# An attention and Fourier kernel: the planner's allowance for late transfers goes by engine instead of by operation

## The chip, the cores and the metric

The kernel runs on one core of a Trainium2 chip. The metric is the device time in microseconds (us), from three runs. A core has TensorE (PE in the profile, its weight loads PEld), VectorE (DVE), ScalarE (ACT), GpSimd (POOL) and SyncE (SP), which here issues every transfer. Each engine works through its own queue in the order in which the program was written for it; engines wait for one another by semaphores.

## The reference

Two independent branches read their own input and their outputs are put side by side: full attention with 32 heads of width 32, and a Fourier mixing layer written as four products with cosine and sine matrices.

```python
# A_x (1, 2048, 1024), wqkv (1024, 3072), wo (1024, 1024)
qkv = (x @ wqkv).reshape(B, S, 3, 32, 32).transpose(2, 0, 3, 1, 4)
scores = einsum("bhqd,bhkd->bhqk", q, k) * 32 ** -0.5
o = einsum("bhqk,bhkd->bhqd", softmax(scores), v)
a = o.transpose(0, 2, 1, 3).reshape(B, S, D) @ wo
# B_x (1, 2048, 1024), dft_seq_* (2048, 2048), dft_hid_* (1024, 1024)
y = einsum("ts,bse->bte", seq_re, x @ hid_re.T) - einsum("ts,bse->bte", seq_im, x @ hid_im.T)
return concatenate([a, y], axis=-1)
```

All is float32.

## The kernel before

**The dense products** (the projections of x to q, k and v, the two Fourier products, the projection with wo) are computed by seven block products where eight would be usual, so many operands are sums or differences of blocks. Each operand goes through the same steps:

- SyncE loads a block of 128x512 numbers, 256 KB (`raw` or `er`; lines 486 and 854), and where a second or third block belongs to it, that one too (`g` or `raw`; line 495).
- An add or subtraction joins them (line 502). GpSimd or VectorE takes it.
- A rounding makes the high part (lines 522 and 523: ScalarE or VectorE); a subtraction of that from the whole makes the low part (line 526: GpSimd or VectorE). They are called `h`, `l` or, together, a `slot`.
- TensorE multiplies high with high, low with high and high with low (lines 416 and 438), 12 or 24 matmuls of 128x512 into one bank of PSUM (`pd` or `psT`). VectorE, in the first steps ScalarE too, evacuates the bank into sums (lines 676 to 792, 979 to 1019; ScalarE's are lines 775 and 790). These matmuls are called fills.

**Attention** runs head by head (heads are counted from 0), three streams at once. S: 32 pairs of score matmuls per head (line 1317), each 128x1024; VectorE takes the negated maximum of each row (`negm`, line 1323) and ScalarE the exponential with its sum (line 1326). Then the maxima of a head are split, transposed on VectorE (lines 1350 to 1360, `lt`), written to HBM (`m_d`) and read back as two more rows of `qs` (`qs<-m_d`, line 1365). T: 64 transposed score matmuls (line 1442), which need those rows, and their exponentials on ScalarE (line 1451). V: runs of matmuls of these with the values (line 1474), 20 to 32 in a row, whose result VectorE evacuates (lines 1494 and 1496).

**The order** is made while the program is built. `Plan` keeps a clock of its own and a time at which each engine is free. An operation (`Op`) names an engine, a cost in us and the operations it follows, and some name a second engine (`other`) that may take it instead. When all that it follows has been started, it is put into the pending list of each engine that may take it, with the time from which it may start; an engine that is free takes the one of the lowest rank among those whose time has come. The order in which the plan starts them is the order of the queues on the chip. An operation that has been put into a queue holds everything behind it there until what it needs is there.

The time from which an operation may start is the end of what it follows, plus 0.1 or 0.2 us, plus an allowance, `SLACK`, that goes by the engine it follows and the engine named first in the operation: 2.0 us after a transfer for GpSimd, VectorE and TensorE, and none for ScalarE. A rounding is named as VectorE's, with ScalarE as the other; ScalarE may take it only while `spare` is set, in the first steps (the first five of the projections' twelve) and in the projection with wo. An add is named as GpSimd's, with VectorE as the other.

TensorE's stream is chosen by the loop at the end. It starts a fill, a pair of S, a T or a run of V. A run of V is held back for up to `PATIENCE` us while work for ScalarE of less than `STOCK` us is waiting; S goes ahead of T while that work is more than `SFIRST`. Fills are handed out in proportion to what attention has done.

Of the kernel before, what the change touches and what calls it, by code (L numbers as in the profile page):

```python
# [38 lines left out]
class Op:  # L39


    __slots__ = ("engine", "cost", "emit", "rank", "kb", "other", "left", "ready", "end", "begun", "then", "soon", "lanes", "two")

    def __init__(self, engine, cost, emit, rank=0.0, kb=0, other=None, two=False):
        self.engine, self.cost, self.emit, self.rank, self.kb, self.other = engine, cost, emit, rank, kb, other
        self.left, self.ready, self.end, self.begun, self.lanes = 0, -1e3, None, False, 1
        self.then, self.soon = [], []
        self.two = two


class Ring:
# [14 lines left out]
class Plan:  # L66
# [5 lines left out]
    LAT_PE = 0.2  # L72
    OVERLAP = {"ACT": 0.15, "DVE": 0.08, "POOL": 0.08}

    SLACK = {("SP", "POOL"): 2.0, ("SP", "DVE"): 2.0, ("SP", "PE"): 2.0, ("POOL", "DVE"): 0.7}
    KB_US = 360.0
    LANDING = 1.6
    QUEUE = 1.0
# [35 lines left out]
    def _wait(self, o, d):  # L114
        if d.end is None:
            d.then.append(o)
            o.left += 1
        else:
            o.ready = max(o.ready, self.after(d, d.engine, o))

    def after(self, d, e, o):
        return d.end + (self.LAT_PE if e == "PE" else self.LAT) + self.SLACK.get((e, o.engine), 0.0)

    def _release(self, o):
        if o.engine != "PE":
            self.seq += 1
            heapq.heappush(self.pending[o.engine], (o.ready, self.seq, o.rank, o))
            if o.other:
                heapq.heappush(self.pending[o.other[0]], (o.ready, self.seq, o.other[2], o))

    def start(self, o, e=None):
        e = e or o.engine
        made = o.emit(e) if o.other else o.emit()
        o.begun = True
        self.free[e] = self.now + (o.cost if e == o.engine else o.other[1])
        if e == "POOL" or e == "DVE" and o.two:
            self.port = self.free[e]
        if e == "DVE" and o.two:
            self.held = made, self.free[e]
        elif e == "POOL" and self.held is not None and self.held[1] > self.now - self.NEAR:  # L140
            self.behind(made, self.held[0])
        if o.kb:
            for _ in range(o.lanes):
                t = max(self.free[e], self.lane[0])
                self.dma = max(self.dma, t) + o.kb / o.lanes / self.KB_US
                o.end = self.dma + self.LANDING
                self.lane = self.lane[1:] + [o.end]
                if o.lanes > 1:
                    self.free[e] = t + o.cost
        else:  # L150
            o.end = self.free[e]
            self.free[e] -= self.OVERLAP.get(e, 0.0)
        for t in o.then:
            t.ready = max(t.ready, self.after(o, e, t))
            t.left -= 1
            if t.left == 0:
                self._release(t)
        for t in o.soon:
            t.ready = max(t.ready, self.now)
            t.left -= 1  # L160
            if t.left == 0:
                self._release(t)
        o.then = o.soon = ()
        o.emit = None
# [56 lines left out]
def kernel(  # L221
# [150 lines left out]
    RES = 400  # L372
    SST = 12
    LEAD = 4
    PATIENCE = 0.5
    STOCK = 1.8
    NEAR = 0.2
    SFIRST = 1
    ADD = 0.68
    FILL = 3 * (7 * 24 * 4 + 7 * 16 * 4 + 7 * 8 * 16 + 2 * 8 * 4)  # L380
    ATT = H * (128 * MM + 16 * PV) + (3 * H2 + 2 * (H - H2)) * SWITCH
# [1 line left out]
    pl = Plan()  # L383
    pl.behind = lambda a, b: tc.add_manual_dep(a.ins, b.ins.name, mybir.DependencyInfo(mybir.DependencyClass.Sync, mybir.DependencyReason.DATA), reason="port")
    op = pl.op
    att_on, t_on = [True], [False]
# [1164 lines left out]
    while nf < len(fills) or any(place[n] < len(s) for n, s in streams.items()):  # L1551
        pl.others()
        if pl.free["PE"] > pl.now:
            pl.now = max(pl.now + 1e-3, min(pl.free["PE"], pl.next_time()))
            continue
        if visit:
            o = visit[0]
            if o.left == 0 and o.ready <= pl.now:
                pl.start(o)
                done += o.cost  # L1560
                visit.pop(0)
            else:
                t = min(pl.next_time(), o.ready if o.left == 0 else 1e18)
                assert t < 1e17, "the plan is stuck"
                pl.idle = getattr(pl, "idle", 0.0) + max(t - pl.now, 1e-3)
                pl.now = max(t, pl.now + 1e-3)
            continue
        heads = {n: s[place[n]] for n, s in streams.items() if place[n] < len(s)}
        if not heads:
            att_on[0] = False  # L1570
        banks = [e for e in banks if e.end is None or e.end + pl.LAT > pl.now]
        room = 0.0
        if len(banks) >= (2 if heads and t_on[0] else 4):
            room = max(pl.now + 1e-3, min([e.end + pl.LAT for e in banks if e.end is not None] or [1e18]))
        ok, times = [], [pl.next_time()]
        waiting = [e for e in waiting if not e.begun]
        stock = max(0.0, pl.free["ACT"] - pl.now) + sum(e.cost for e in waiting)
        held = False
        if "S" in heads and "T" in heads and heads["T"][0].left == 0:
            th, tk = heads["T"][1:3]  # L1580
            held = heads["S"][2] / 33.0 * SST + 16 * (heads["S"][1] - th - 1) - tk / 4 > LEAD
        for n, (o, h, k, *_) in heads.items():
            if o.left:
                continue
            ready = o.ready + LATE
            if n == "V":
                ready = max(ready, room)
            if ready > pl.now:
                times.append(ready)
                continue  # L1590
            if n == "V":

                near = any(m in heads and heads[m][0].left == 0 and heads[m][0].ready + LATE < pl.now + NEAR and not (m == "S" and held) for m in "ST")
                if (near or stock < STOCK) and pl.now < o.ready + PATIENCE:
                    times.append(o.ready + PATIENCE)
                    continue
            rank = {"V": 0, "T": 1, "S": 0.5 if stock > SFIRST else 1.5}[n]
            if n == "S" and "T" in heads and heads["T"][0].left == 0:
                th, tk = heads["T"][1:]
                lead = k / 33.0 * SST + 16 * (h - th - 1) - tk / 4  # L1600
                if lead > LEAD:
                    continue
                if lead > 0:
                    rank = 2
            ok.append((rank, n))
        fill = None
        if nf < len(fills):
            o, first, left = fills[nf]
            ready = o.ready if o.left == 0 else 1e18
            if first:  # L1610
                ready = max(ready, room)
            if ready + (LATE if first else 0.0) <= pl.now:
                fill = o
            elif ready < 1e17:
                times.append(ready + LATE)
        if fill is not None and (not ok or (not first and left <= HB) or nf / (FILL - RES) <= done / ATT):
            pl.start(fill)
            nf += 1
            if first:
                banks.append(frees[ng])  # L1620
                ng += 1
            continue
        if ok:
            n = min(ok)[1]
            o = heads[n][0]
            pl.start(o)
            place[n] += 1
            t_on[0] = t_on[0] or n == "T" or n == "S" and place["S"] > 31
            if n == "V":
                banks.append(heads[n][2])  # L1630
                visit = list(heads[n][3])
            elif o in exp_of:
                waiting.append(exp_of[o])
            done += o.cost
            continue
        t = min(times)
        assert t < 1e17, "the plan is stuck"
        pl.idle = getattr(pl, "idle", 0.0) + max(t - pl.now, 1e-3)
        pl.now = max(t, pl.now + 1e-3)
    while True:  # L1640
        pl.others()
        t = pl.next_time()
# [31 lines left out]
```

## Time and profile before

| | us |
| --- | --- |
| median of three runs | 2944.36 |
| lowest and highest | 2943.4 and 2950.26 |
| the profiled execution's own time | 2947.49 |
| its span, first to last instruction | 2945.7 |
| TensorE busy in the span | 2933.7 |
| VectorE, ScalarE, GpSimd busy | 2300.6, 2271.9, 907.5 |

The span is what the views of the profile cut into pieces; the 1.8 us between it and the execution's own time lie around it. A row of the timeline or of the chain of waits has its start and its length in us. In rows of groups the numbers behind the bar are the busy time, the mean of one in ns, and the idle time of the engine just before them with what ended it. A row "A <- B: x, n, y" of the waits says that A's engine was idle x us in total, n times, y at the longest, until B. Rows of the stages give the length of the stage, then the busy time of PE, PEld, DVE, ACT and POOL, the clock granted to TensorE, the share of the transfer engines and GB/s.

### The profile page before, as it was taken

To read this page: it belongs to the slowest core of one execution; us is meant where nothing else is said; L and a number is where in the kernel's file an instruction comes from. 1 tells how busy PE (TensorE), PEld (TensorE's weight loads), DVE (VectorE), ACT (ScalarE), POOL (GpSimd) and SP (SyncE) were. 2 spreads that over 40 slices of the span, in tenths; PEclk is the share of its full clock that TensorE was granted. 3 is DMA by queue.
4 is the path that set the end of the run, shared out by engine and by line. 5 is a ranking of instruction groups with operands and counts; after the bars stand their busy time and mean duration, and the time that the engine had idled before them with its cause. 6 is when DMAs were issued, how large, how long until landed. Compare 5 with 4: busy or idle time off the path is not lost.

```text
span 2945.7 us, 45665 instructions
## 1 busy us (share of the span) xinstructions
PE 2933.7 (100%) x14922; PEld 2149.6 (73%) x14922; DVE 2300.6 (78%) x3141; ACT 2271.9 (77%) x4321; POOL 907.5 (31%) x709
## 2 busy tenths in 40 slices
PE   9999999999999999999999999999999999999999
PEld 7887777677777777777777777776777766776787
DVE  6778888678877877777678888888777888887685
ACT  4348888888888888888888888888988888886331
POOL 2323336222213332232112543333122444342142
PEclk9999999999999999999999999999999999999999
DMA  9975658667636655665434776565434786655753
GB/s 349 365 237 182 193 184 286 208 214 236 219 109 225 215 177 166 206 231 166 140 111 154 244 230 199 184 195 153 135 112 133 220 264 215 198 179 181 241 201 127
DMA packets 393881, 587.97 MB, mean 200 GB/s; under 512 B 112782, under 2 KB 114574, under 8 KB 393518
## 3 DMA queue, kind: packets, MB, share of 16 engines
q1 hardware_dynamic: 393644, 585.05, 61.8%
q8 instruction: 120, 1.97, 0.3%
q14 instruction: 117, 0.96, 0.1%
HBM read 421.30 MB, written 163.59 MB: 199 GB/s over the span
## 4 chain that ended last, share of the span: by engine, by line
PE 96%; DMA 2%; DVE 1%; SPq 0%; issue 0%; ACT 0%; POOL 0%; DVEq 0%; ACTq 0%
PE pd L416 44%; PE psT L1442 16%; PE psS L1317 16%; PE pd L1474 15%; PE psT L416 6%; DMA qs<-m_d 0%; DVE negm L1323 0%; DMA er<-in_wqk 0%; PE psT L438 0%; DMA g<-in_wqk 0%; DMA raw<-in_wqk 0%; DMA er<-in_xa 0%; DMA g<-in_ct 0%; DMA ks<-qk_d 0%; DVE l L526 0%
## 5 line engine op out<-in xcount | busy, mean ns | idle before, releaser
L1323 DVE TENSOR_REDUCE negm<-psS 128x1 f32<-128x1024 f32 x1024 | 1242.1, 1220 | 239.6 <-PE psS L1317 234.1
L1326 ACT ACTIVATE psS<-psS,negm 128x1024 f32<-128x1024 f32 x1024 | 1219.1, 1190 | 134.3 <-DVE negm L1323 128.7
L416 PE MATMUL pd<-slot,h 128*128 128x512 f32 x3360 | 1147.2, 390 | 0.2 <-DVE ot L1496 0.2
L1451 ACT ACTIVATE pt<-psT 128x512 f32<-128x512 f32 x1296 | 775.0, 695 | 212.5 <-PE psT L1442 201.6
L1442 PE MATMUL psT<-qs,ks 128*128 128x512 f32 x2048 | 793.5, 393 | 1.2 <-DMA qs<-m_d 1.0
L416 PEld LDWEIGHTS pd<-slot,h 128*128 128x128 f32 x3360 | 630.8, 188 | 132.3 <-DVE ot L1496 0.6
L416 PE MATMUL pd<-slot,l 128*128 128x512 f32 x1680 | 654.6, 390 | 0.0
L1317 PE MATMUL psS<-ks,qs 128*128 128x512 f32 x1552 | 473.5, 390 | 1.9 <-ACT psS L1326 1.8
L1442 PEld LDWEIGHTS psT<-qs,ks 128*128 128x128 f32 x2048 | 379.8, 188 | 128.1 <-issue 41.8
L526 POOL TENSOR_TENSOR l<-raw,h 128x512 fp32r<-128x512 f32 x163 | 210.2, 1290 | 728.0 <-PE psT L1442 346.6
L502 POOL TENSOR_TENSOR raw<-raw,g 128x512 f32<-128x512 f32 x225 | 291.9, 1304 | 392.5 <-DVE raw L502 66.2
L416 PEld LDWEIGHTS pd<-slot,l 128*128 128x128 f32 x1680 | 315.4, 188 | 66.8 <-issue 0.8
L1474 PE MATMUL pd<-pt,vt 128*32 128x512 f32 x2592 | 345.8, 594 | 0.4 <-DVE slot L979 0.4
L1317 PEld LDWEIGHTS psS<-ks,qs 128*128 128x128 f32 x1552 | 290.5, 188 | 66.6 <-ACT psS L1326 4.7
L526 POOL TENSOR_TENSOR slot<-raw,slot 128x512 fp32r<-128x512 f32 x174 | 223.8, 1292 | 368.1 <-DVE slot L523 101.5
L1326 ACT ACTIVATION_READ_ACCUMULATOR psS<-psS,negm 128x1 f32 x1024 | 316.6, 309 | 0.0
L1451 ACT ACTIVATE ptm<-psT 128x512 f32<-128x512 f32 x392 | 237.5, 701 | 39.1 <-PE psT L1442 38.4
L1451 ACT ACTIVATE ptl<-psT 128x512 f32<-128x512 f32 x360 | 221.8, 705 | 35.2 <-PE psT L1442 33.2
L1474 PEld LDWEIGHTS pd<-pt,vt 128*32 128x32 f32 x2592 | 89.4, 110 | 180.9 <-issue 173.0
L416 PE MATMUL pd<-slot,slot 128*128 128x512 f32 x768 | 193.7, 390 | 0.0
L416 PEld LDWEIGHTS pd<-slot,slot 128*128 128x128 f32 x768 | 144.2, 188 | 31.0
L523 DVE CAST h<-raw 128x512 fp32r<-128x512 f32 x321 | 148.9, 465 | 16.8 <-PE pd L416 14.2
(138 smaller groups left out, 2362.5 us busy)
## 6 DMA issues: line engine op xcount, KB each, us to landing
raw<-in_ct SPq DMA_DIRECT2D x224, 256.0 KB
g<-in_ct SPq DMA_DIRECT2D x128, 256.0 KB
c<-u_d SPq DMA_DIRECT2D x120, 256.0 KB
qk_d<-e SPq DMA_DIRECT2D x52, 512.0 KB
qs<-qk_d SPq DMA_DIRECT2D x128, 192.0 KB
ks<-qk_d SPq DMA_DIRECT2D x128, 192.0 KB
raw<-ab_d SPq DMA_DIRECT2D x96, 256.0 KB
g<-ab_d SPq DMA_DIRECT2D x80, 256.0 KB
```

Of the source, the lines that this page charges most:

```text
L416: nc.tensor.matmul(box["ps"], a[1]((a[0].hi, a[0].lo)[u]()), b[1]((b[0].hi, b[0].lo)[v]()), start=k == 0, stop=k == n - 1)
L502: return (nc.gpsimd if e == "POOL" else nc.vector).tensor_tensor(out=dest(), in0=dest() if a is None else a.get(), in1=other["q"] if "q" i ...
L523: return nc.vector.tensor_copy(hi(), raw())
L526: return (nc.gpsimd if e == "POOL" else nc.vector).tensor_tensor(out=lo(), in0=raw(), in1=f(hi()), op=ALU.subtract)
L1317: nc.tensor.matmul(p[:, i * NB : i * NB + NB], (QX[0] if own else QS[h % 2])[:, qt * P : qt * P + P], KS[h % 2][:, c * 1024 + i * NB : c * ...
L1323: nc.vector.tensor_reduce(out=ST["negm"][:, c, qt : qt + 1], in_=box["p"], axis=AX.X, op=ALU.max, negate=True)
L1326: nc.scalar.activation(box["p"], box["p"], AF.Exp, bias=ST["negm"][:, c, qt : qt + 1], accum_out=ST["sums"][:, c, qt : qt + 1])
L1442: nc.tensor.matmul(box["p"], KS[h % 2][:, t * P : t * P + P], QS[h % 2][:, j * NB : j * NB + NB], start=True, stop=True)
L1451: nc.scalar.activation(box["t"], box["p"], AF.Exp)
L1474: nc.tensor.matmul(po["p"][j * DH : j * DH + DH, :], VT[h][:, k, :], box["t"], start=(k == t0), stop=(k == t), tile_position=(0, j * DH),)
```

## The change

The allowance after a transfer is taken out of `SLACK` (TensorE's alone stays there) and put into `MARGIN`, by the engine that may take the operation: 2 for GpSimd, 2 for VectorE, 0 for ScalarE. An operation now remembers when the last transfer that it follows has landed (`landed`), and each of its engines has it in its pending list with its own time. While attention is under way, VectorE's margin is 3. Three constants of TensorE's loop change with it.

```diff
-    SLACK = {("SP", "POOL"): 2.0, ("SP", "DVE"): 2.0, ("SP", "PE"): 2.0, ("POOL", "DVE"): 0.7}
+    SLACK = {("SP", "PE"): 2.0, ("POOL", "DVE"): 0.7}
+    MARGIN = {"POOL": 2, "DVE": 2, "ACT": 0}
...
             o.ready = max(o.ready, self.after(d, d.engine, o))
+            if d.engine == "SP":
+                o.landed = max(o.landed, d.end)
...
-            heapq.heappush(self.pending[o.engine], (o.ready, self.seq, o.rank, o))
-            if o.other:
-                heapq.heappush(self.pending[o.other[0]], (o.ready, self.seq, o.other[2], o))
+            for e, rank in ((o.engine, o.rank), *([(o.other[0], o.other[2])] if o.other else [])):
+                heapq.heappush(self.pending[e], (max(o.ready, o.landed + self.MARGIN.get(e, 0.0)), self.seq, rank, o))
...
             t.ready = max(t.ready, self.after(o, e, t))
+            if e == "SP":
+                t.landed = max(t.landed, o.end)
...
-    PATIENCE = 0.5
-    STOCK = 1.8
+    PATIENCE = 2
+    STOCK = 2.4
     NEAR = 0.2
-    SFIRST = 1
+    SFIRST = 0.3
...
             att_on[0] = False
+        pl.MARGIN["DVE"] = 3 if heads and t_on[0] else 2
```

The lines of the changed kernel stand five further down (six from the last loop on): line 502 is 507 there, 522 and 523 are 527 and 528, 526 is 531, 1323 is 1328.

The change moves instructions on all engines. Three places:

ScalarE's queue at the start of the program, from the roundings of the second half of x (slot32 to slot35) on; `acc` is an evacuation of TensorE's first groups. Before:

```order
L522 ACTIVATE slot32_663<-er_603 128x512
L522 ACTIVATE slot33_670<-er_615 128x512
L522 ACTIVATE slot34_678<-er_623 128x512
L522 ACTIVATE slot35_686<-er_632 128x512
L790 ACTIVATE acc0_694<-psT_599 128x512
L790 ACTIVATE acc2_699<-pd_607 128x512
L522 ACTIVATE slot36_705<-er_640 128x512
L522 ACTIVATE slot37_712<-er_647 128x512
```

And in the changed kernel:

```order
L527 ACTIVATE slot32_640<-er_595 128x512
L527 ACTIVATE slot33_648<-er_606 128x512
L527 ACTIVATE slot34_656<-er_614 128x512
L527 ACTIVATE slot35_665<-er_626 128x512
L527 ACTIVATE slot36_673<-er_634 128x512
L527 ACTIVATE slot37_681<-er_643 128x512
L527 ACTIVATE slot38_689<-er_651 128x512
L795 ACTIVATE acc1_699<-pd_597 128x512
L527 ACTIVATE slot39_705<-er_659 128x512
```

Three roundings have come ahead of the first evacuation, the evacuations of the first and the third group have gone to VectorE, and that of the second has come to ScalarE. In SyncE's queue the three loads of `raw` that stood in the 9th to 11th place have moved behind these loads, so that `er_651` is the 15th load, as `er_632` was.

VectorE's queue late in attention, under the scores of head 28, around the two adds for one block of the sequence matrix (stored as s2_d5_3). Before, they stand between the maxima:

```order
L523 CAST h_26253<-raw_25999 128x512
L526 TENSOR_TENSOR l_26258<-raw_25999,h_26253 128x512
L1323 TENSOR_REDUCE negm_25967<-psS_26250 128x1
L502 TENSOR_TENSOR raw_26108<-raw_26108,g_26211 128x512
L1323 TENSOR_REDUCE negm_25967<-psS_26278 128x1
L502 TENSOR_TENSOR raw_26108<-raw_26108,g_26239 128x512
L1323 TENSOR_REDUCE negm_25967<-psS_26301 128x1
L523 CAST h_26329<-raw_26102 128x512
```

In the changed kernel the adds for the same block (raw_26198) are in GpSimd's queue:

```order
L507 TENSOR_TENSOR raw_26070<-raw_26070,g_26192 128x512
L507 TENSOR_TENSOR raw_26091<-raw_26091,g_26207 128x512
L531 TENSOR_TENSOR l_26327<-raw_26070,h_26315 128x512
L507 TENSOR_TENSOR raw_26198<-raw_26198,g_26274 128x512
L507 TENSOR_TENSOR raw_26198<-raw_26198,g_26296 128x512
L531 TENSOR_TENSOR l_26399<-raw_26091,h_26368 128x512
L507 TENSOR_TENSOR raw_26242<-raw_26242,g_26358 128x512
```

Both have gone from VectorE to GpSimd, as have 70 of the 147 adds raw<-raw,g of VectorE in the whole program.

VectorE's queue after the last maximum of head 1 (the first row), up to the transpose `lt` that its m_d transfer sends. Before:

```order
L1323 TENSOR_REDUCE negm_2716<-psS_3510 128x1
L523 CAST slot1_3533<-raw_3346 128x512
L1350 TENSOR_REDUCE lh_3540<-negm_2716 128x16
L1346 TENSOR_REDUCE nm_3543<-negm_2716 128x16
L1323 TENSOR_REDUCE negm_3535<-psS_3537 128x1
L1323 TENSOR_REDUCE negm_3535<-psS_3566 128x1
L676 TENSOR_TENSOR slot15_2517<-slot15_2517,pd_3504 128x512
L1323 TENSOR_REDUCE negm_3535<-psS_3589 128x1
L1353 TENSOR_TENSOR lh_3540<-nm_3543,lh_3540 128x16
L1379 TENSOR_TENSOR tt_3613<-nm_3543,negm_2716 128x16 x2
L1360 STREAM_TRANSPOSE lt_3621<-lh_3540 128x32
```

And in the changed kernel:

```order
L1328 TENSOR_REDUCE negm_2716<-psS_3505 128x1
L1355 TENSOR_REDUCE lh_3533<-negm_2716 128x16
L1351 TENSOR_REDUCE nm_3535<-negm_2716 128x16
L528 CAST slot1_3537<-raw_3346 128x512
L1328 TENSOR_REDUCE negm_3528<-psS_3530 128x1
L1358 TENSOR_TENSOR lh_3533<-nm_3535,lh_3533 128x16
L1384 TENSOR_TENSOR tt_3565<-nm_3535,negm_2716 128x16 x2
L1365 STREAM_TRANSPOSE lt_3571<-lh_3533 128x32
```

Two maxima of the next head and one evacuation no longer stand ahead of the transpose.

More of the change, by code (lines that the diff above doesn't have):

```diff
@@ L39 @@
 class Op:
-    __slots__ = ("engine", "cost", "emit", "rank", "kb", "other", "left", "ready", "end", "begun", "then", "soon", "lanes", "two")
+    __slots__ = ("engine", "cost", "emit", "rank", "kb", "other", "left", "ready", "end", "begun", "then", "soon", "lanes", "two", "landed")
     def __init__(self, engine, cost, emit, rank=0.0, kb=0, other=None, two=False):
@@ L48, in __init__ @@
         self.two = two
+        self.landed = -1e3
 class Ring:
```

## The prediction

> **What bounds the kernel now.** First the page: busy time by engine, and the chain that ended last.
>
> ```profile
> span 2945.7 us, 45665 instructions
> PE 2933.7 (100%) x14922; PEld 2149.6 (73%) x14922; DVE 2300.6 (78%) x3141; ACT 2271.9 (77%) x4321; POOL 907.5 (31%) x709
> PE 96%; DMA 2%; DVE 1%; SPq 0%; issue 0%; ACT 0%; POOL 0%; DVEq 0%; ACTq 0%
> ```
>
> TensorE is busy for all but 2945.7 - 2933.7 = 12.0 us, and the chain runs through it for 96%. The change alters no matmul: both orders hold 12,874 of them (the trace records the 2,048 with V twice) in the same 72 runs with V. So only those 12.0 us can shrink; they can also grow without limit. The next views ask where they lie: the stages (us of the stage; its length, TensorE's busy time) and TensorE's own waits (us in total, times, longest).
>
> ```profile
> 0.00:20.00 20.00, 16.68 (x62) 12.86 (x63) 10.54 (x18) 11.05 (x19) 6.96 (x9) 1.00 0.89 303
> 20.00:312.00 292.00, 292.00 (x1328) 236.05 (x1327) 227.19 (x314) 161.61 (x287) 88.79 (x69) 1.00 0.80 278
> 312.00:324.00 12.00, 11.57 (x75) 6.08 (x74) 11.38 (x25) 6.16 (x14) 5.98 (x6) 1.00 0.90 272
> 324.00:2700.00 2376.00, 2371.69 (x12333) 1703.26 (x12333) 1884.43 (x2546) 2011.94 (x3866) 746.21 (x581) 1.00 0.60 190
> 2700.00:2946.00 246.00, 241.78 (x1130) 191.38 (x1128) 167.09 (x242) 81.13 (x141) 59.60 (x46) 1.00 0.55 186
> ...
> PE psS L1317 <- ACT psS L1326: 3.0, 3, 1.1
> PE psT L438 <- ACT acc L790: 1.7, 1, 1.7
> PE pd L1550 <- DVE qs L298: 1.5, 1, 1.5
> PE psT L1442 <- DMA qs<-m_d: 1.0, 2, 0.6
> PE pd L1474 <- DVE slot L979: 0.4, 1, 0.4
> ```
>
> The start costs 3.3 us, the last stage 4.2 (nearly all of it the store after the last matmul), and 4.7 lie between, in attention (0.4 and 4.3). The clock is 1.00 throughout. A matmul row shows 390 ns, yet
>
> ```profile
> 2762.46 10.88 PE psT L416 x48
> ```
>
> gives 10.88 / 48 = 0.227 us from one to the next; a gap under 0.39 - 0.227 = 0.16 us is therefore unseen, and a seen one is 0.16 longer than shown. With that, the waits that a new order could remove are at most 4.7 + 1.9 at the start + some 1.5 unseen = 8 us. A measurement of this kernel tells about 0.3%, 8.8 us, from no change. A clear gain is nearly out of reach; a clear loss is not.
>
> **The three waits of the scores.** The plan's allowance is meant for transfers that land late, so each wait is followed back. The third, at 2395 us:
>
> ```profile
> 2390.91 2.94 DMA raw<-in_ct
> 2393.86 0.69 DVE raw L502
> 2394.56 1.15 DVE negm L1323
> 2395.79 1.21 ACT psS L1326 x2
> 2397.04 0.73 PE psS L1317 x2
> ```
>
> Here VectorE itself stands before an add whose transfer is late; the maximum behind it, the exponential and the next scores are all late with it. The other two, at 1651 and 1995 us, look alike to TensorE but start on GpSimd:
>
> ```profile
> 1647.60 4.43 POOL L502 TENSOR_TENSOR raw<-raw,g 128x512 f32<-128x512 f32 x3 [1.39 <-DMA raw<-ab_d]
> 1647.73 1.44 DVE L523 CAST h<-raw 128x512 fp32r<-128x512 f32 x1
> 1649.21 1.67 DVE L526 TENSOR_TENSOR l<-raw,h 128x512 fp32r<-128x512 f32 x1
> ...
> 1991.38 2.73 POOL L502 TENSOR_TENSOR raw<-raw,g 128x512 f32<-128x512 f32 x2 [1.71 <-DMA raw<-t_d]
> ```
>
> GpSimd waited for a transfer, ran its adds late, and VectorE's rounding and subtraction then ran beside them and took 1.44 and 1.67 us. The means of both forms are 465 and 719 ns:
>
> ```profile
> L523 DVE CAST h<-raw 128x512 fp32r<-128x512 f32 x321 | 148.9, 465 | 16.8 <-PE pd L416 14.2 <-PE psT L416 1.4 <-DMA raw<-in_wqk 0.8
> L526 DVE TENSOR_TENSOR l<-raw,h 128x512 fp32r<-128x512 f32 x158 | 112.8, 719 | 3.1
> L502 DVE TENSOR_TENSOR raw<-raw,g 128x512 f32<-128x512 f32 x147 | 107.1, 734 | 28.3 <-DMA raw<-ab_d 6.2 <-DMA raw<-in_ct 5.7 <-issue 5.6
> L502 POOL TENSOR_TENSOR raw<-raw,g 128x512 f32<-128x512 f32 x225 | 291.9, 1304 | 392.5 <-DVE raw L502 66.2 <-issue 51.9 <-DMA raw<-t_d 43.5
> ```
>
> **The change, part by part, against the profiled execution (2947.49 us).**
>
> *VectorE's allowance, 3 instead of 2 in attention.* The order of the changed kernel has 77 of the adds raw<-raw,g on VectorE and 295 on GpSimd, against 147 and 225: 70 are moved. The two that stood at 2394 us on VectorE are among them. VectorE's wait for late transfers loses its way to TensorE: the one wait of 1.0 us goes, with 0.16 unseen: -1.2. It could be 0 (another add takes its place; 77 stay), and no more than -1.2, since only this one reached TensorE.
>
> *The same 70 adds on GpSimd.* Its allowance stays at 2, and its adds made the other two waits (3.0 - 1.0 = 2.0 us, with the unseen part 2.3). Scaled by the adds, 2.3 x 70 / 225 = +0.7. Below, 0: GpSimd idles two thirds of the span, and no row has TensorE waiting for GpSimd itself. Above: its waits for these transfers are
>
> ```profile
> POOL raw L502 <- DMA raw<-t_d: 43.5, 7, 18.0
> POOL raw L502 <- DMA raw<-in_ct: 39.3, 11, 8.7
> POOL raw L502 <- DMA raw<-ab_d: 37.0, 11, 9.8
> ```
>
> 29, of which two reached TensorE. 70 more adds make 29 x 70 / 225 = 9 more; if every one cost TensorE the mean 1.0 + 0.16 us, +10.4. I take 0.7, since 27 of 29 were covered by the other matmuls that the plan had placed there. The load itself, 70 x 1.304 = 91 us for GpSimd less what it hands back elsewhere (its operations rise by 37 in all), is hidden in its idle time; if it were not, the weights of the dense products would come late and TensorE would show waits for line 531, of which there are none today.
>
> The Trainium skill (GPSIMD Engine Reference, Engine selection) says elementwise work belongs on VectorE, GpSimd being about twice as slow for two inputs. The rows agree: 1304 / 734 = 1.8. By that rule the move is a loss, 70 x (1.304 - 0.734) = 40 us more of engine time; the first rival below is what it would make of the end. The skill (SBUF — State Buffer, SBUF: two separate sides) also calls the pair of ports that both share an exclusive lock, held for the whole instruction; the 1.44 and 1.67 us beside GpSimd's adds fit, and by it each further GpSimd add is one more chance of such a collision.
>
> *PATIENCE, STOCK, SFIRST.* They move the scores of the next head against the runs of 32 matmuls with V, and so the time that the statistics of a head have to reach SBUF through HBM (m_d). TensorE waited for that twice:
>
> ```profile
> 319.40 4.04 DMA qs<-m_d
> 553.76 4.49 DMA qs<-m_d
> ```
>
> Between a head's last score and its first transposed score stand 70 matmuls for head 1 and 57 for head 4 before; 51 and 71 in the changed order; over all heads 55 before and 63 now in the mean. Head 4 gains 14 x 0.227 = 3.2 us and its wait of 0.6 goes. Head 1 loses some 4 us of lead, but its statistics also come sooner: VectorE has two maxima and one evacuation less ahead of them, and the maxima alone each stand behind a pair of scores that comes every 2 us:
>
> ```profile
> 309.17 1.23 DVE L1323 TENSOR_REDUCE negm<-psS 128x1 f32<-128x1024 f32 x1 [0.27 <-PE psS L1317]
> 311.21 1.22 DVE L1323 TENSOR_REDUCE negm<-psS 128x1 f32<-128x1024 f32 x1 [0.81 <-PE psS L1317]
> ```
>
> That is about 4 us, so it stays as it was. Together -0.8 with the unseen part; from -1.3 (both go) to +4 (head 1 loses its lead and the chain is no shorter). The one wait of 0.4 for a bank (L979) may go or come again: 0.
>
> *ScalarE's roundings without allowance.* They stand only in the first 290 us and after attention. At the start the queue of ScalarE decides:
>
> ```profile
> 9.99 5.27 DMA er<-in_xa
> ...
> 15.28 0.63 ACT L522 ACTIVATE slot<-er 128x512 fp32r<-128x512 f32 x1 [0.16 <-DMA er<-in_xa]
> 15.81 0.58 ACT L790 ACTIVATE acc<-psT 128x512 f32<-128x512 f32 x1
> ...
> 16.45 0.50 PE L438 MATMUL psT<-slot,h 128*128 128x512 f32 x1 [1.69 <-ACT acc L790]
> ```
>
> An evacuation waits behind the rounding of the 15th load, TensorE behind the evacuation. In the changed order three roundings more stand ahead of ScalarE's first evacuation, but three loads of raw have left the queue ahead of them: the last of these roundings again needs the 15th load. So 0. Bounds: -1.9 (the evacuations of VectorE alone decide) to +1.9 (it doubles). After the last run with V there are 833 matmuls instead of 818 to cover the projection's loads, 15 x 0.227 = 3.4 us more cover: 0 there.
>
> **The sum** is -1.2 + 0.7 - 0.8 = -1.3 us, or 2946.2 for the profiled execution. That one was 3.1 us above the median of the three runs, 2944.36; the same 1.3 off the median gives 2943.1, so 2943.
>
> **The rivals.**
>
> *GpSimd becomes the late engine (slower).* All nine further waits reach TensorE: +10.4 - 1.2 - 0.8 = +8.4, and with one more wait of 1.2 for head 1, +9.6, 2954. It decides from the point where 11 of GpSimd's some 38 waits for transfers come through to TensorE, instead of 2 of 29: (8.8 + 1.2 + 0.8) / 1.16 = 9 further ones. For it: both collisions above are GpSimd's, its allowance is not raised, and it is in order, so one late add holds the next. Against it: the cover of 27 in 29. 0.17.
>
> *All movable waits of attention go (faster).* 4.7 and some 1.3 unseen: -6.0, 2938.4. For it: the changed order is more even, mostly 76 or 77 dense matmuls between runs with V where it was 73 to 92. Against it: the transfers land as late as before, and two of its six waits, GpSimd's, are of a kind that it doesn't touch. 0.10, of which 0.04 below 2935.5.
>
> *The change does nothing that can be seen.* VectorE's longest sums of waits for a transfer are the 6.2 and 5.7 us in its row above, and one wait reached TensorE; a new order deals as many new ones elsewhere: 2944.4, from 2941 to 2949. 0.25.
>
> **How the numbers follow.** The forecast, 2943 (2940 to 2946), has 0.48. Faster by over 0.3% (below 2935.5) needs more than all of the movable waits: 0.04. Slower by over 0.3% (above 2953.2) is the first rival: 0.17. The rest, 0.79, is no change. The range runs from 2938, the second rival's value, to 2954, where the first rival's bounds end.
>
> **What would show it.** VectorE's rows for L507 with a quarter as many waits for transfers as now, and no TensorE wait that starts in them; GpSimd's x295 with some 38 waits for transfers; rows of 1.4 to 1.7 us for L528 and L531 beside GpSimd's adds; at most three waits of the scores for ScalarE; at the start again one wait near 1.7 us, ended by an evacuation; the wait for qs<-m_d at head 4 gone. The forecast is wrong if TensorE's busy time moves by more than a few us at all, if its idle time exceeds 20 us, or if waits for line 531 or 527 appear on it.

## The result, and the profile after

| | before | changed |
| --- | --- | --- |
| median, us (22 runs each) | 2945.96 | 2940.96 |
| lowest and highest | 2942.92 and 2950.26 | 2939.14 and 2942.71 |
| span of the profiled execution | 2945.7 | 2940.6 |
| TensorE idle in the span | 12.0 | 9.1 |
| adds raw<-raw,g on VectorE / GpSimd | 147 / 225 | 77 / 295 |
| VectorE's idle time ahead of these adds | 28.3 | 3.3 |

The ratio is 0.9983, 95% interval 0.9976 to 0.9990: 5.0 us or 0.17% less, under the 0.3% from which the prediction calls a difference one. These 22 runs resolve it all the same: the slowest of the changed kernel, 2942.71 us, lies below the fastest of the kernel before, 2942.92 us.

First the page of the changed kernel, busy time by engine and the chain that ended last:

```profile
span 2940.6 us, 45778 instructions
PE 2931.5 (100%) x14922; PEld 2151.9 (73%) x14922; DVE 2275.1 (77%) x3103; ACT 2271.7 (77%) x4322; POOL 956.6 (33%) x746
PE 98%; DVE 1%; DMA 1%; ACT 0%; SPq 0%; issue 0%; DVEq 0%; ACTq 0%
```

The matmuls are the same 14,922 records. Then the stages (length, then the busy time of PE, PEld, DVE, ACT and POOL, clock, DMA share, GB/s):

```profile
0.00:20.00 20.00, 17.21 (x63) 13.19 (x64) 13.12 (x22) 14.21 (x23) 6.96 (x9) 1.00 0.86 291
20.00:312.00 292.00, 292.00 (x1329) 236.19 (x1328) 223.27 (x314) 158.43 (x284) 86.91 (x68) 1.00 0.82 280
312.00:324.00 12.00, 12.00 (x79) 6.85 (x77) 11.37 (x21) 6.74 (x13) 5.08 (x5) 1.00 0.89 275
324.00:2700.00 2376.00, 2373.49 (x12351) 1708.12 (x12348) 1864.16 (x2509) 2020.21 (x3880) 792.33 (x616) 1.00 0.60 190
2700.00:2941.00 241.00, 236.84 (x1110) 187.57 (x1108) 163.19 (x240) 72.09 (x124) 65.32 (x51) 1.00 0.55 190
```

Beside the same stages before: TensorE's idle time at the start went from 3.3 to 2.8 us, in the twelve us around head 1 from 0.4 to 0, in the rest of attention from 4.3 to 2.5, and in the last stage, counted to the end of the span, from 3.9 to 3.8. And TensorE's waits in the changed kernel (us in total, times, longest):

```profile
PE pd L1555 <- DVE qs L303: 1.5, 1, 1.5
PE psT L443 <- DVE acc L799: 1.3, 1, 1.3
PE psT L1447 <- DMA qs<-qk_d: 1.3, 1, 1.3
PE psS L1322 <- ACT psS L1331: 1.2, 3, 0.5
```

The scores still wait three times, but 0.5 us at most. Both waits for m_d are gone, and so are the three small ones behind L979, L1496 and L522. One has come: a transposed score of head 2 waits for a load of q. The chain there, and under it SyncE's row for this load and the two before it:

```profile
395.18 5.64 DMA qs<-qk_d
400.82 0.05 issue
400.87 0.71 PE psT L1447 x2
```

```profile
394.25 3.59 SPq L315 DMA_DIRECT2D qs<-qk_d  x3
```

From issue at 395.18 us to landing the load took 5.64 us. Of the 3.59 us in which SyncE issued the three, the first two took 0.42 each and this one 2.66; why is open.

Waits do not hold the whole difference. From the start times of all matmul records one can take the distance from each to the next and subtract the shortest distance of its kind (0.227 us for a fill or a score; a run with V as a whole). What is left over, in us:

| | before | changed | difference |
| --- | --- | --- | --- |
| sum of shortest distances, start and tail | 2920.7 | 2920.7 | 0.0 |
| excess in distances over 0.15 us too long | 9.1 | 5.5 | -3.6 |
| excess in distances 0.025 to 0.15 us too long | 10.7 | 9.0 | -1.6 |
| excess below that | 5.2 | 5.3 | +0.1 |
| span | 2945.7 | 2940.6 | -5.2 |

(The last figures are rounded.) The middle row, some 110 small delays before and 90 after, is of the size of all waits that the view shows, and no row of the waits has it. What causes these delays is open.

So the mechanism that the change is made of can be seen in the trace: VectorE hardly stands before late adds any more. Whether the 5 us come from it is another question, and the experiments are about that.

### The profile page after: what moved, and what is told of

Read it like the earlier page. It is cut to its first block, busy times and chain, and to the rows that moved or that the text cites. A ratio compares the mean times of both kernels' runs of the same rounds, so it can differ in the third digit from the quotient of the medians.

```text
span 2940.6 us, 45778 instructions
## 1 busy us (share of the span) xinstructions
PE 2931.5 (100%) x14922; PEld 2151.9 (73%) x14922; DVE 2275.1 (77%) x3103; ACT 2271.7 (77%) x4322; POOL 956.6 (33%) x746
## 4 chain that ended last, share of the span: by engine, by line
PE 98%; DVE 1%; DMA 1%; ACT 0%; SPq 0%; issue 0%; DVEq 0%; ACTq 0%
PE pd L421 44%; PE psT L1447 16%; PE psS L1322 16%; PE pd L1479 15%; PE psT L421 6%; DVE negm L1328 0%; DMA er<-in_xa 0%; DVE l L531 0%; DMA qs<-qk_d 0%; PE psT L443 0%; ACT psS L1331 0%; DVE h L528 0%; PE pd L443 0%; ACT slot L527 0%; DVE slot L531 0%
## 5 line engine op out<-in xcount | busy, mean ns | idle before, releaser
L507 POOL TENSOR_TENSOR raw<-raw,g 128x512 f32<-128x512 f32 x295 | 382.6, 1304 | 483.8 <-DVE l L531 63.8
L531 POOL TENSOR_TENSOR l<-raw,h 128x512 fp32r<-128x512 f32 x157 | 202.5, 1290 | 554.6 <-PE psT L1447 236.6
L531 POOL TENSOR_TENSOR slot<-raw,slot 128x512 fp32r<-128x512 f32 x156 | 201.0, 1293 | 518.0 <-DVE slot L528 146.3
```

Of the source, the lines that this page charges most:

```text
L507: return (nc.gpsimd if e == "POOL" else nc.vector).tensor_tensor(out=dest(), in0=dest() if a is None else a.get(), in1=other["q"] if "q" i ...
L531: return (nc.gpsimd if e == "POOL" else nc.vector).tensor_tensor(out=lo(), in0=raw(), in1=f(hi()), op=ALU.subtract)
```

## The experiments

Three theories. **A**: the allowance does it, since VectorE and what queues behind it are no longer held by late transfers. **B**: the three constants of TensorE's loop (`PATIENCE`, `STOCK`, `SFIRST`) do it. **C**: neither does; each edit makes the planner deal a wholly new order, every order has its own few collisions (instructions of two engines that hold one another up), and this one happens to have fewer. All runs were compared with the kernel before on the same chip, in five rounds each (11 runs of the kernel); the kernel before had medians of 2945.78, 2946.25 and 2945.96 us there.

### One part alone

**The constants alone**, in the kernel before:

```diff
-    PATIENCE = 0.5
-    STOCK = 1.8
+    PATIENCE = 2
+    STOCK = 2.4
...
-    SFIRST = 1
+    SFIRST = 0.3
```

> The kernel before with the three constants alone (PATIENCE 2, STOCK 2.4, SFIRST 0.3), allowances as before: 135 adds raw<-raw,g on VectorE, 237 on GpSimd. If the allowance does the work (A): within 1.5 us of before, TensorE's waits for the scores still about 3 us. If the constants do it (B), by a more even order of the runs with V: 3 to 5 us faster than before, most of the gain. If the gain is the luck of a newly dealt order (C): anywhere from 4 us faster to 4 us slower.

Measured: 2945.7 us, ratio 1.0002 (0.9993 to 1.0011). Nothing is gained by this order, though its scores wait for ScalarE 1.6 us in all instead of 3.0.

**The allowance alone**, the changed kernel with the three constants of before:

```diff
-    PATIENCE = 2
-    STOCK = 2.4
+    PATIENCE = 0.5
+    STOCK = 1.8
...
-    SFIRST = 0.3
+    SFIRST = 1
```

> The change without the three constants: 81 adds on VectorE, 291 on GpSimd. A: 3 to 5 us faster than before, TensorE's waits for the scores at most half of 3.0 us. B: within 1.5 us of before. C: anywhere from 4 us faster to 4 us slower, in no relation to e1.

Measured: 2947.44 us, ratio 1.0005 (0.9996 to 1.0014). The profile says that the mechanism is there in full; the group of VectorE's adds in this kernel (busy time, mean ns, idle time ahead of them):

```profile
L507 DVE TENSOR_TENSOR raw<-raw,g 128x512 f32<-128x512 f32 x81 | 62.5, 781 | 6.6 <-POOL raw L507 6.6
```

None of VectorE's idle time ahead of them is put down to a transfer, and still nothing is gained. TensorE's three longest sums of waits in the same kernel, and under them the chain of waits and the timeline around one of the five waits of the scores:

```profile
PE psS L1322 <- ACT psS L1331: 3.3, 5, 1.3
PE pd L1555 <- DVE qs L303: 1.5, 1, 1.5
PE psT L1447 <- DMA qs<-m_d: 1.0, 2, 0.7
...
```

```profile
1601.43 1.46 DVE h L528
1602.90 0.02 issue
1602.92 1.67 DVE l L531
1604.59 1.15 DVE negm L1328
...
1605.82 1.21 ACT psS L1331 x2
1607.03 0.04 issue
1607.08 0.73 PE psS L1322 x2
```

```profile
1601.31 2.73 POOL L507 TENSOR_TENSOR raw<-raw,g 128x512 f32<-128x512 f32 x2 [8.06 <-issue]
1601.43 1.45 DVE L528 CAST h<-raw 128x512 fp32r<-128x512 f32 x1
1602.92 1.67 DVE L531 TENSOR_TENSOR l<-raw,h 128x512 fp32r<-128x512 f32 x1
```

A rounding and a subtraction run beside two adds of GpSimd and take 1.46 and 1.67 us; the maximum, the exponential and the scores behind them are late. It is the collision that the prediction showed at 1651 and 1995 us in the kernel before. The chain of this kernel has the same piece, a subtraction of 1.66 to 1.74 us and then a maximum, an exponential and scores, six times between 1600 and 2513 us. Four of the five waits (2.7 of the 3.3 us) stand behind one of these; the fifth, 0.6 us, behind ScalarE's own work. So with VectorE's own waits gone, GpSimd's collisions alone make nearly as much waiting of the scores as the 3.0 us that there were. Not all of it is GpSimd's lateness: the profile puts its idle time ahead of the adds down to a transfer in three of the six cases, and to nothing that it shows in the others, as at 1601 us. A and B alone both lose ground by this; but each kernel is one order, and how much the orders scatter was not known yet.

**VectorE's allowance back at 2**, all else as changed:

```diff
-        pl.MARGIN["DVE"] = 3 if heads and t_on[0] else 2
+        pl.MARGIN["DVE"] = 2
```

> The change with VectorE's allowance at 2 in attention too: 160 adds on VectorE, 212 on GpSimd. A: the gain goes, within 1.5 us of before, and waits of VectorE for transfers at its adds come back (before: about 28 us of idle time ahead of them). B: the gain stays, 4 to 6 us faster than before. C: no telling.

Measured: 2946.68 us, ratio 1.0000 (0.9992 to 1.0009). 160 adds are on VectorE, which is idle 46.9 us ahead of them. The gain is away, as A would have it, but C allows that too.

**ScalarE's allowance back at 2**, all else as changed:

```diff
-    MARGIN = {"POOL": 2, "DVE": 2, "ACT": 0}
+    MARGIN = {"POOL": 2, "DVE": 2, "ACT": 2}
```

> The change with ScalarE's allowance at 2: the same 77 and 295 adds, only the start and the projection differ. A and B: the gain stays, 4 to 6 us faster than before; TensorE's wait at the start stays within 0.5 us of 1.7. C: it stays too, since the order in attention is nearly the same one. More than 2 us slower than the change would show that ScalarE's part carries some of the gain.

Measured: 2940.94 us, ratio 0.9985 (0.9976 to 0.9994): all of the gain is there. This edit leaves TensorE's order in attention as it is: when the records are merged into rows by line and tile name (without buffer numbers), only two of 7,885 rows differ, both among the first 115. So the part for ScalarE's roundings brings nothing, and the gain lies in what the two orders share, attention above all. It also shows that nearly one order, built twice, gives one time. The single waits are less fixed than the time: in e4's profile the scores wait at other places in part (1.8 us, 1.0 at the longest), and head 2's wait for the load of q is not there. Its three loads were issued in 1.35 us:

```profile
393.94 1.35 SPq L315 DMA_DIRECT2D qs<-qk_d  x3
```

### The same rules, dealt anew

C has a test of its own. `LATE`, 0.15 us, is what TensorE's loop adds to the time from which an operand counts as ready. A shift by 10 or 20 ns has nothing to do with transfers or with the constants, but moves the order: counted in the same merged rows of TensorE, a line-by-line comparison of e4 with the changed kernel has 4 lines that differ, the deals with another `LATE` have 738 to 2,368 against the kernel that they come from, and the change itself has 2,117 against the kernel before.

```diff
-    LATE = 0.15
+    LATE = 0.16
```

> The changed kernel with the plan's LATE at 0.16 us instead of 0.15: ten ns that mean nothing for the chip, but deal the order anew (62 adds on VectorE, 310 on GpSimd). If allowance and constants together make the gain (A+B): 2939 to 2943, as the change. If the change is one lucky deal among many (C): around before's 2945 to 2947, or anywhere within 4 us of it.

Measured: 2945.55 us, 1.0000 (0.9991 to 1.0008). The same edit to 0.14:

> The changed kernel with LATE at 0.14 us: another deal (82 adds on VectorE, 290 on GpSimd). A+B: 2939 to 2943. C: anywhere within 4 us of before, and not the same as e5.

Measured: 2944.3 us, 0.9994 (0.9985 to 1.0002). Then both in the kernel before, 0.16 first:

> The kernel before with LATE at 0.16 us (148 adds on VectorE, 224 on GpSimd). A+B: within 1.5 us of before, since neither part is in it. C: anywhere within 4 us of before, also as fast as the change.

Measured: 2946.64 us, 0.9998 (0.9989 to 1.0007). With 0.14:

> The kernel before with LATE at 0.14 us (144 adds on VectorE, 228 on GpSimd). A+B: within 1.5 us of before. C: anywhere within 4 us of before. The four runs of this call together give the spread that a new deal alone makes: under 1 us for A+B, 2 us or more for C.

Measured: 2947.94 us, 1.0007 (0.9998 to 1.0016). A shift of 10 ns that means nothing takes 3 to 5 us off the gain. But all three deals of the changed rules lay below all three of the old, so a systematic part of some 3 us stayed possible; four more deals were made for that. The changed rules with 0.17:

> The changed kernel with the planner's LATE 0.17 instead of 0.15, a shift of 20 ns in its reckoning that has nothing to do with the allowance: a third new deal of the same rules. So far the changed rules gave 2941.0 (as it stands), 2945.6 and 2944.3 us, the old rules 2946.0, 2946.6 and 2947.9. Theory 'a systematic part is left' (changed rules about 3 us better on the mean of the deals): 2942 to 2945. Theory 'luck alone' (both rules deal from one distribution, mean some 2945.5): 2943 to 2949, as likely above 2946 as below.

Measured: 2945.12 us, 0.9998 (0.9989 to 1.0007). With 0.13:

> The changed kernel with LATE 0.13: a fourth new deal of the changed rules. 'A systematic part is left': 2942 to 2945. 'Luck alone': 2943 to 2949. Both theories: TensorE's waits are some 3 to 8 us in all, with the same kinds as before (scores for ScalarE, a load, a column) at other places.

Measured: 2948.97 us, 1.0009 (1.0001 to 1.0018), the slowest of all. The old rules with 0.17:

> The kernel before with LATE 0.17: a third new deal of the old rules. 'A systematic part is left': 2946 to 2949, above every deal of the changed rules. 'Luck alone': 2941 to 2948, one of these two kernels below 2945.

Measured: 2944.87 us, 0.9996 (0.9987 to 1.0004). With 0.13:

> The kernel before with LATE 0.13: a fourth new deal of the old rules. 'A systematic part is left': 2946 to 2949. 'Luck alone': 2941 to 2948. With five deals of each rule the two means differ by 3 us or more by the first theory, and by less than 1.5 us by the second.

Measured: 2945.53 us, 1.0001 (0.9992 to 1.0010).

All deals together. The waits and the idle time come from each kernel's one profiled execution, the time from its runs:

| rules | `LATE` | VectorE idle ahead of adds raw<-raw,g | TensorE's waits, sum | median, us |
| --- | --- | --- | --- | --- |
| changed | 0.13 (e10) | 1.7 | 7.4 | 2948.97 |
| changed | 0.14 (e6) | 3.3 | 4.9 | 2944.30 |
| changed | 0.15 (the change) | 3.3 | 5.3 | 2940.96 |
| changed | 0.16 (e5) | 5.3 | 8.0 | 2945.55 |
| changed | 0.17 (e9) | 0.7 | 5.3 | 2945.12 |
| old | 0.13 (e12) | 23.8 | 4.8 | 2945.53 |
| old | 0.14 (e8) | 13.4 | 7.4 | 2947.94 |
| old | 0.15 (before) | 28.3 | 8.0 | 2945.96 |
| old | 0.16 (e7) | 18.3 | 7.9 | 2946.64 |
| old | 0.17 (e11) | 21.3 | 5.8 | 2944.87 |

The mean of the changed rules is 2945.0 us, that of the old ones 2946.2. The difference of 1.2 us stands against a standard error of 1.4 (the five of each scatter by 2.9 and 1.2). It is in the range that was set for luck alone before the last four deals, under 1.5 us, and not in the 3 us or more of a systematic part. VectorE's idle time falls by the rules, from 13 to 28 us to 1 to 5, without an exception; the time does not go with it. Nor does it go with the sum of the listed waits: 4.8 to 5.3 us of them stand beside 2940.96 us (the change) and beside 2944.30 to 2945.53 (e6, e9, e12). TensorE's three longest sums of waits in the worst deal, e10:

```profile
PE psS L1322 <- ACT psS L1331: 3.3, 9, 1.3
PE pd L1555 <- DVE qs L303: 1.5, 1, 1.5
PE psT L443 <- DVE acc L799: 1.4, 1, 1.4
...
```

The scores wait nine times. The longest, 1.3 us, is no collision; here VectorE itself waits for a late add of GpSimd:

```profile
338.42 1.29 POOL L507 TENSOR_TENSOR raw<-raw,g 128x512 f32<-128x512 f32 x1 [12.16 <-DMA raw<-in_wqk]
339.74 0.43 DVE L528 CAST h<-raw 128x512 fp32r<-128x512 f32 x1 [2.11 <-POOL raw L507]
```

Seven of the others, 1.7 us together, stand behind an instruction of VectorE that was drawn out beside an add of GpSimd, and one of 0.3 behind ScalarE. These sums are no larger than before's (3.0) or e2's (3.3), so they do not explain why this deal is the slowest. In its group of adds GpSimd has 301, and 61 us ahead of them end with transfers of one matrix alone:

```profile
L507 POOL TENSOR_TENSOR raw<-raw,g 128x512 f32<-128x512 f32 x301 | 387.3, 1296 | 437.9 <-DMA raw<-in_ct 61.2 <-issue 60.9 <-DMA raw<-ab_d 50.6
```

C explains the 5 us best: the changed kernel's time is repeatable (e4), but it is that of its order, which other deals of the same rules do not have. That it is fast because it has fewer of the listed collisions, the second half of C, is not shown. What stays open is a systematic part: its likeliest size is the 1.2 us, and five deals of each kind leave room, at 95%, from a gain of 4.7 to a loss of 2.3 us. The same scatter holds for e1, e2 and e3, one deal each: they show that neither part brings the 5 us whatever the order, not that it brings nothing in the mean.

## Why the prediction was right, step by step

**What bounds the kernel.** Right: no matmul changed, the sum of the shortest distances is equal to 0.1 us in both kernels, and only the 12.0 us of idle time and what lies unseen beside it moved. TensorE's busy time moved by 2.2 us, which is the unseen part. The prediction gave that part too little room: it put "some 1.5 unseen" into its 8 us of movable waits, while the small delays alone made 10.7 us before.

**VectorE's allowance (-1.2).** The wait at 2395 us is gone and no wait of the scores starts at an add of VectorE. The group of those adds in the changed kernel:

```profile
L507 DVE TENSOR_TENSOR raw<-raw,g 128x512 f32<-128x512 f32 x77 | 55.5, 728 | 3.3 <-POOL raw L507 1.8 <-DMA g<-in_ct 1.3 <-issue 0.2
```

One wait of 1.3 us ahead of them is put down to a transfer, where 18 (22.3 us) stood before and a quarter was predicted: the direction was right, and stronger.

**The 70 adds on GpSimd (+0.7).** The prediction had some 38 waits for the three kinds of transfers; there are 9 + 21 + 12 = 42, as GpSimd's own waits in the changed kernel show:

```profile
POOL raw L507 <- DMA raw<-in_ct: 41.9, 21, 6.1
POOL raw L507 <- DMA raw<-ab_d: 37.1, 12, 6.5
POOL raw L507 <- DMA raw<-t_d: 29.5, 9, 9.2
```

Three waits of the scores are left, the number that was allowed for, and the collision behind them is the predicted one; the chain before the longest, and GpSimd's adds beside it:

```profile
2505.26 1.66 DVE l L531
2506.92 1.15 DVE negm L1328
...
2508.15 1.21 ACT psS L1331 x2
2509.36 0.04 issue
2509.40 0.73 PE psS L1322 x2
```

```profile
2503.66 2.72 POOL L507 TENSOR_TENSOR raw<-raw,g 128x512 f32<-128x512 f32 x2 [0.69 <-DMA raw<-ab_d]
2504.45 0.78 DVE L528 CAST h<-raw 128x512 fp32r<-128x512 f32 x1 [0.20 <-PE pd L421]
2505.26 1.66 DVE L531 TENSOR_TENSOR l<-raw,h 128x512 fp32r<-128x512 f32 x1
```

GpSimd waited 0.69 us for a transfer and its two adds ran until 2506.38 us; the subtraction, which began beside the second, ended 0.54 us later. In e2's rows above the adds end at 1604.04 and the subtraction at 1604.59, 0.55 later. The Trainium skill (SBUF — State Buffer, SBUF: two separate sides) says that of the two engines the one that comes second waits for the whole of the other's instruction; the trace agrees, as most of the subtraction's usual 0.7 us lies after the add's end. What was off is the price: 1.2 us for three waits, where two of GpSimd's had cost 2.0. Both terms together were put at -0.5 and came out at some -1.8 (3.0 to 1.2 shown).

**The constants (-0.8).** Head 4's wait for m_d is gone, as predicted. That of head 1 was to stay and is gone too. SyncE's rows for its m_d before, and in the changed kernel, and then head 1's first transposed score there:

```profile
314.87 0.54 SPq L1364 DMA_DIRECT2D m_d<-lt  x1
319.40 0.22 SPq L1365 DMA_DIRECT2D qs<-m_d  x1
```

```profile
310.72 0.53 SPq L1369 DMA_DIRECT2D m_d<-lt  x1
313.73 0.26 SPq L1370 DMA_DIRECT2D qs<-m_d  x1
```

```profile
318.07 0.39 PE L1447 MATMUL psT<-qs,ks 128*128 128x512 f32 x1
```

The store leaves 4.15 us sooner, the "about 4" of the prediction. The lead shrank as predicted, too: from head 1's last score to its first transposed score are 11.8 us now, and were 16.8 with a wait of 0.4 shown and 0.16 unseen, so 4.4 less. What the prediction did not have is the load, which leaves 5.7 us sooner, since it follows the store by 3.0 us instead of 4.5; that was just enough, and the transposed score waits for nothing. So m_d gave its 1.0 us and the 0.3 unseen. But the new wait for a load of q at head 2 took 1.3 + 0.16 back, and that was in no term.

**The start (0).** Instead of one wait of 1.7 ended by an evacuation of ScalarE there is one of 1.3 ended by an evacuation of VectorE (line 799); the stage idles 0.5 us less. e4 has ScalarE's evacuation at the end of that wait again, also 1.3 us, and the same total time: the edit for ScalarE is worth nothing that shows, as the sum had it.

**The sum (-1.3) is the step that was mis-sized.** Measured: -5.2 in the profiled executions, -5.0 in the medians. Worked out again: scores -1.8, m_d -1.3, the load of q +1.5, the three small waits (which the sum left at 0, saying of one that it may go or come) -0.8 and 0.5 unseen, the long wait at the start -0.4, together -3.3, beside the 3.6 measured; and -1.6 in the small delays that no view of waits lists. This account holds for one execution of each kernel; e4 shows that some of its waits change places. The sum's deeper fault is shown by the experiments. The sum treats each term as the price of an edit, but the terms are waits of one order: e2 has the whole of the first term's mechanism, with none of the gain; e1 has the constants and gains nothing; and a shift of 10 ns in `LATE` moves the time as much as all terms together. The frame of the third rival, that a new order deals as many waits elsewhere, fits the ten deals (2941 to 2949, the very range it was given); the changed kernel lies at the good end of it.

**That 2940 to 2946 holds the measured time is luck in part.** The prediction took its 1.3 us off 2944.36, the median of three runs; 22 runs of the same kernel have 2945.96. From there the same sum gives 2944.7, and with 3 us to either side 2941.7 to 2947.7, which would not hold 2940.96. The wider range, from 2938, holds it either way.

**The other rivals.** The first, GpSimd as the late engine, does not decide in the changed kernel, but parts of its mechanism are seen in e2 and in e10, with 2.7 and 2.9 us of the scores' waits behind GpSimd instead of 10: most of the late adds stay covered. The second, all movable waits gone, came near in time (2938.4) but not in kind, since four waits in attention are left.

## What to carry to other kernels

Where an order is made by a planner and the bound engine is already busy to half a per cent, judge a rule by several deals of it: shift a constant that means nothing and compare the means, since one build against one build measures the deal. That a mechanism is visible in the trace (25 us of idle time gone from an engine) says nothing of the time as long as those waits were covered; and of a change in two parts, run each part alone before crediting either.

## What the runs showed that was not expected

- The order alone moves this kernel by 8 us (2940.96 to 2948.97 us in five deals of the changed rules), while the kernel before, measured anew beside each group of runs on at least three chips, had medians within 0.5 us of each other (2945.78 to 2946.25).
- Delays of 25 to 150 ns between matmuls, about 100 in each kernel, make up 9.0 to 11.5 us. That is as much as or more than all waits that the view lists (4.8 to 8.0 us), and they move with the order too.
